# First product of an attention + feed-forward kernel: direct sums before, Strassen's 7 block products from the third chunk on

## The chip, the cores and the metric

One NeuronCore of a Trainium2 chip. The metric is the device time of one execution in microseconds (us). Before the change it was 1001.22 us (median of 3 runs, 1000.88 to 1002.4).

## What is computed

`q`, `k`, `v` are (8 batches, 8 heads, 576 tokens, 64). Each head has two attentions, and their outputs are added: one over tokens pooled by 4 (144 of them), repeated 4 times, and one in a band of 7 neighbours. The sum is laid out as `x` with 4608 rows (tokens) of 512, and then goes through a feed-forward layer without biases:

```python
h = x @ w_in                      # (4608, 512) @ (512, 2048): the first product
g = np.where(h >= 1, h, np.where(h <= -1, 0.0, (h + 1) ** 2 / 4))
return (g @ w_out).astype(np.float32)   # (4608, 2048) @ (2048, 512): the second product
```

All is in fp32. Each factor of the two large products is split into a high part in the fp32r format and the remainder ("low part", fp32r as well), and a product is the sum of three matmuls: high by high, low by high, high by low.

## The kernel before, in words

**Units of work.** The 2048 columns of `h` are cut into 16 slices `f` of 128. The tokens are cut into chunks `c`: 512, 256, and ten of 384. For each (chunk, slice) there is one step of the first product, `mm1` (L648): 12 matmuls 128x128 by 128 x chunk (4 blocks of the 512 input columns, 3 matmuls each, L663) into one PSUM bank. Then comes the activation with the split of its result (L675 to L696): Relu and Square on ScalarE, max/min on VectorE (L688), high part on ScalarE (L690), low part on VectorE (L695; on GpSimd in the first chunk, L692). Then `mm2` (L699) adds the slice's part of the second product into the chunk's output banks: for each 128 tokens 3 matmuls 128 x 512 (L714). After the last slice ScalarE copies the output to SBUF (L719) and SP's queue stores it (L720).

**Attention.** 32 units, one for each batch and pair of heads ("attention pair", L293): some 50 small matmuls in six steps (L369, L393, L493, L511, L534, L552) with VectorE, ScalarE and GpSimd work in between (GpSimd: L426, L479, L480). From the third batch on a pair uses the PSUM banks 0 to 2 (`shares`, L347). The last steps add the two attentions in PSUM (L577) and write the high and the low part of `x` (L592 on ScalarE, L597 on VectorE) into two rings of 1152 tokens, `xh` and `xl`.

**Weights.** `w_in` and `w_out` come from HBM as 64-bit words of doubles' bits, 512 KB for each slice and matrix (L619), and are converted on ScalarE and VectorE during the first chunk (L623 to L640). All 32 converted tiles then stay in SBUF.

**Order.** Nothing is ordered by hand: a planner (`Plan`, L81) has a cost, a due time (`key`) and the buffers of each operation, plays them through and writes out one fixed order for each engine; on the chip each engine, and SP's queue of transfers, goes through its own list in that order. `mm1` runs some 11 us ahead of `mm2` (`lead`). Attention of the first batch stands ahead of all, that of the second beside the first chunk, later ones beside the chunk ahead of the one that needs them.

## Time and profile before

| | |
|---|---|
| Median of the runs | 1001.22 us |
| The profiled execution's own time | 999.11 us |
| Its span, first to last instruction | 997.3 us |
| TensorE clock granted, mean over the span | 0.991 |
| PE / VectorE / ScalarE / GpSimd busy | 97% / 51% / 49% / 12% of the span |
| Moved by DMA | 66.23 MB |

The profile is one execution. PE is TensorE's matmuls, PEld its weight loads (they overlap matmuls), DVE VectorE, ACT ScalarE, POOL GpSimd, SP the queue that issues the transfers. Matmuls are pipelined: a row's duration is longer than the distance to the next row, and the price of a matmul is the distance from start to start. L with a number is a line of the kernel. A row of a timeline has start, duration, engine, line, operation, out<-in, shape, and how many were merged; a row of a window has its length and then each engine's busy time and count, the granted clock, the DMA engines' busy share and GB/s; a row of the groups has total, mean in ns, idle time before and what ended it.

### The profile page before, as it was taken

Reading aid. Unit: us, or ns where it says so; the run is one execution under the profiler, and the core shown is the slowest. Engines: PE = TensorE matmul, PEld = TensorE weight load, DVE = VectorE, ACT = ScalarE, POOL = GpSimd, SP = SyncE. Lnnn points to the kernel's source line nnn. Section 1 sums busy time; section 2 is a strip of 40 time slices with the busy share of each in tenths; the row PEclk is TensorE's granted clock in tenths of the full one; section 3 lists DMA queues with packets and bytes.
Section 4 is the critical chain, followed back from the end, with each engine's and each line's share of the span. In section 5 each row is a group of like instructions: output and inputs, shape, how many; then the busy total and the mean of one; then the engine's idle time right before and its main releaser. Section 6 shows DMA issues by size and latency. Waiting matters only on the chain.

```text
span 997.3 us, 18271 instructions
## 1 busy us (share of the span) xinstructions
PE 965.8 (97%) x7620; PEld 831.5 (83%) x7620; DVE 505.0 (51%) x908; ACT 485.3 (49%) x1063; POOL 123.5 (12%) x120
## 2 busy tenths in 40 slices
PE   7799999999999999999999999999999999999998
PEld 5577778888888888998887888998888888899997
...
DMA packets 26531, 66.23 MB, mean 66 GB/s; under 512 B 3152, under 2 KB 3152, under 8 KB 26448
## 3 DMA queue, kind: packets, MB, share of 16 engines
...
q14 instruction: 23, 0.19, 0.1%
...
## 4 chain that ended last, share of the span: by engine, by line
PE 84%; DVE 8%; ACT 3%; DMA 2%; issue 1%; SPq 0%; ACTq 0%; DVEq 0%
PE ps L714 38%; PE ps L663 37%; PE ps L369 2%; PE ps L511 2%; PE ps L493 2%; PE ps L534 2%; PE ps L552 1%; ACT sp L450 1%; PE ps L393 1%; DMA raw_i<-w_in 1%; DVE m L630 1%; DVE ps L460 1%; DMA vp<-vp 1%; DVE m L628 1%; DVE xl L597 1%
## 5 line engine op out<-in xcount | busy, mean ns | idle before, releaser
L663 PE MATMUL ps<-xh,w_i 128*128 128x384 f32 (+2 forms) x1536 | 396.3, 340 | 7.0 <-DVE gl L695 4.8
L714 PE MATMUL ps<-w_o,gh 128*128 128x512 f32 x1152 | 369.5, 402 | 0.5 <-DVE w_o L639 0.5
L663 PEld LDWEIGHTS ps<-xh,w_i 128*128 128x128 f32 x1536 | 275.2, 188 | 31.7 <-DVE gl L695 10.4
L663 PE MATMUL ps<-xl,w_i 128*128 128x384 f32 (+2 forms) x768 | 258.8, 337 | 0.0
L714 PEld LDWEIGHTS ps<-w_o,gh 128*128 128x128 f32 x1152 | 207.3, 188 | 43.0 <-issue 9.5
L714 PE MATMUL ps<-w_o,gl 128*128 128x512 f32 x576 | 227.4, 395 | 0.0
L688 DVE SCALAR_TENSOR_TENSOR ps<-ps,u 128x384 f32<-128x384 f32 (+1 forms) x176 | 96.5, 548 | 257.9 <-ACT u L680 257.9
L675 ACT ACTIVATE u<-ps 128x384 f32<-128x384 f32 (+2 forms) x192 | 94.4, 492 | 255.3 <-PE ps L663 255.3
L695 DVE TENSOR_TENSOR gl<-ps,gh 128x384 fp32r<-128x384 f32 (+1 forms) x176 | 95.9, 545 | 107.6 <-PE ps L714 64.3
L663 PEld LDWEIGHTS ps<-xl,w_i 128*128 128x128 f32 x768 | 144.6, 188 | 2.9
L690 ACT CAST gh<-ps 128x384 fp32r<-128x384 f32 (+1 forms) x176 | 83.1, 472 | 109.0 <-DVE ps L688 106.6
L714 PEld LDWEIGHTS ps<-w_o,gl 128*128 128x128 f32 x576 | 108.2, 188 | 25.2
L680 ACT ACTIVATE u<-u 128x384 f32<-128x384 f32 (+2 forms) x192 | 100.8, 525 | 6.0
L426 POOL TENSOR_TENSOR sl<-sl,mxl 128x640 f32<-128x640 f32 x24 | 30.3, 1261 | 468.5 <-DVE mxl L424 468.5
L479 POOL TENSOR_TENSOR vh<-vp 72x512 f32<-72x512 f32 x32 | 41.4, 1295 | 133.0 <-ACT u L675 57.9
L450 ACT ACTIVATE sp<-ps,mxp 128x144 f32<-128x144 f32 x96 | 36.4, 380 | 28.2 <-DVE ps L460 14.1
L421 DVE TENSOR_TENSOR sl<-ps,band_sb 128x640 f32<-128x640 f32 x24 | 19.8, 825 | 55.4 <-PE ps L393 49.5
L428 ACT ACTIVATE sl<-sl 128x640 f32<-128x640 f32 x32 | 23.6, 737 | 37.0 <-POOL sl L426 28.4
L460 DVE TENSOR_REDUCE ps<-sl 128x10 f32<-128x640 f32 x32 | 26.4, 826 | 16.1 <-ACT sp L450 13.8
L511 PE MATMUL ps<-ident,sp 128*72 128x128 f32 x192 | 27.4, 281 | 5.8 <-ACT al L499 5.1
L692 POOL TENSOR_TENSOR gl<-u,gh 128x512 fp32r<-128x512 f32 x16 | 22.6, 1411 | 78.8 <-ACT gh L690 61.1
L592 ACT CAST xh<-ps 128x576 fp32r<-128x576 f32 x32 | 20.4, 639 | 22.2 <-DVE ps L577 22.1
...
## 6 DMA issues: line engine op xcount, KB each, us to landing
...
```

Of the source, the lines that this page charges most:

```text
L426: o_s = op("POOL", 1.3, lambda: nc.gpsimd.tensor_tensor(slf(), slf(), ml_n(), op=ALU.subtract), [o_m], [slb, mlb], kk[2], name=name + "sub ...
L450: nc.scalar.activation(spb.tile[:, i], sp_view()[:, i] if i < 2 else sp_other(), AF.Exp, bias=mxb.tile[:, i : i + 1], scale=scale, accum_o ...
L460: o_su = op("DVE", 0.825, lambda: nc.vector.tensor_reduce(sums()[:, 0:NB], slf(), axis=AX.X, op=ALU.add), [o_e, o_sp], [slb, spp], kk[4], ...
L479: nc.gpsimd.tensor_tensor(vhb.tile, vpb.tile[:, :, 0:2, :], vpb.tile[:, :, 2:4, :], op=ALU.add)
L511: nc.tensor.transpose(tp_v[:, kb, i, :], spb.tile[:, i, kb * KB : (kb + 1) * KB], ident if i < 2 else swapped,)
L663: nc.tensor.matmul(h, wi[:, wt, cc * P : (cc + 1) * P], xt[:, cc, ts], start=(i == 0), stop=(i == 3 * NCC - 1))
L675: o2 = op("ACT", 0.49 + e, lambda: nc.scalar.activation(u(), h(), AF.Relu, bias=0.5, scale=0.5), [o1], [hb, ub], key, name=f"relu {c},{f}" ...
L680: nc.scalar.activation(u(), u(), AF.Square)
L688: o4 = op("DVE", 0.556 + e * 1.2, lambda: nc.vector.scalar_tensor_tensor(g(), h(), 1.0, u(), op0=ALU.max, op1=ALU.min), [o3], [hb, ub], ke ...
L690: o5 = op("ACT", 0.50 + e, lambda: nc.scalar.copy(ghb.tile[:, :n], g()), [o4], [held, ghb], key, name=f"gh {c},{f}")
L695: o6 = op("DVE", 0.556 + e * 1.2, lambda: nc.vector.tensor_tensor(glb.tile[:, :n], g(), ghb.tile[:, :n], op=ALU.subtract), [o5], [held, gh ...
L714: nc.tensor.matmul(o, g.tile[:, ts], wb.tile[:, wt, :], start=f == 0 and i == 0, stop=f == NFC - 1 and i == 2)
```

## The change

The chunks become nine of 512 tokens. The first two still use the direct product. From the third on two slices `f1`, `f2` = 2j, 2j+1 are taken together, and the 256x512 by 512x512 product is made of 2x2 blocks with Strassen's scheme in Winograd's form: A11, A12, A21, A22 are the blocks of the two slices' weights (slice, half of the 512 input columns), B11 to B22 those of `x` (half of the columns, half of the tokens). With S1 = A21+A22, S2 = S1-A11, S3 = A11-A21, S4 = A12-S2 and T1 = B12-B11, T2 = B22-T1, T3 = B22-B12, T4 = B21-T2 there are seven products (A11 B11, A12 B21, S2 T2, S3 T3, S1 T1, A22 T4, S4 B22) in place of eight. Each is 6 matmuls of 128x128 by 128x256 (L883).

- **Products** (`winograd`): they go by turns into two PSUM banks G and H, of which half is used. Two add on top of what stands there (S2 T2 and S1 T1 on A11 B11), S4 B22 as well. Between them ScalarE copies a bank to SBUF three times (L889), and VectorE adds a bank to such a copy three times (L892). The two banks change roles from one j to the next; the next j's first product waits for both.
- **Activation** (`hidden`): on four quarters of 256 tokens by 128 columns for each j instead of on whole chunks. Three quarters have their source in SBUF (`tt`), one in PSUM. The second product keeps its shape: 8 x 3 matmuls 128x512 for each j (L833).
- **Sums of x** (`sums_of_x`): attention writes `x` as fp32 into a ring `xr` of 1024 tokens (L591); for each chunk VectorE makes the four T (L688), ScalarE the high and VectorE the low parts of seven operands (L705, L706). L592 and L597 of before are gone. The first two chunks get plain high and low parts (`parts`).
- **Sums of weights** (`sums_of_weights`, `stored`): once for each j, beside the second chunk, VectorE makes S1 to S4 (L731), with high and low parts (L753); they and A11, A12, A22 are stored to HBM: A1 512 KB, A22 256 KB, S12 512 KB, S34 512 KB. Each chunk from the third on loads them again (L861), into 8 places of SBUF where w_in of the slices 0 to 7 had been; the operands of x take 12 places, 8 of them of w_in's slices 8 to 15.
- **Banks**: outputs have the banks 4 to 7, G and H the banks 2 and 3, attention the banks 0 and 1 (`shares` is off).
- The planner's due times and costs are set anew (`K`), and it now can give one operation several buffers of a pool.

The core of the diff (the lines of the changed kernel in the text above are those of its own numbering):

```diff
-RING = 2 * S
-
-CHUNKS = [(0, 512), (512, 256)] + [(t, 384) for t in range(768, NT, 384)]
-NCH = len(CHUNKS)
+TOK = 512
+NCH = NT // TOK
+DIRECT = 2
+RING = 2 * TOK
+HALF = TOK // 2
...
-    xh = cpool.tile([P, NCC, RING], F32R, name="xh")
-    xl = cpool.tile([P, NCC, RING], F32R, name="xl")
+    xr = cpool.tile([P, NCC, RING], F32, name="xr")
+    tt = cpool.tile([P, NT1, HALF], F32, name="tt")
+    gt = cpool.tile([P, NG1, 2 * HALF], F32R, name="gt")
     ps = ppool.tile([P, 8, 512], F32, name="ps")
+    dpool = ctx.enter_context(tc.tile_pool(name="dram", bufs=1, space=bass.MemoryType.DRAM))
...
-        shares = b > 1
+        shares = False
...
+                nc.vector.tensor_tensor(
+                    xr[:, p, r : r + m].rearrange("p (s f) -> p s f", f=FACTOR),
+                    pl_s()[:, s0 : s0 + m].rearrange("p (s f) -> p s f", f=FACTOR),
+                    xdb.tile[:, s0 // FACTOR : (s0 + m) // FACTOR].unsqueeze(2).broadcast_to([P, m // FACTOR, FACTOR]),
+                    op=ALU.add,
...
+        war = [o for c in range(NCH) if TOK * c <= S * b + S - RING - 1 for o in x_read[c][p]] if b > 1 else []
+        o_x = op("DVE", 0.755, add, [o_xd] + war, [plp, xdb], kk[9], name=name + "x")
+        x_done[b, p] = o_x
...
+    def parts(c):
+        for kt in range(NCC):
+            pb = sbuf("x", [P, 2, TOK], F32R, "w", [32 + kt])
+            src = xr[:, kt, r0 : r0 + TOK]
+            o1 = op("ACT", 0.62, lambda pb=pb, src=src: nc.scalar.copy(pb.tile[:, 0], src), deps, [pb], key + 0.3 * kt, name=f"xh {c},{kt}")
+            o2 = op("DVE", 0.69, lambda pb=pb, src=src: nc.vector.tensor_tensor(pb.tile[:, 1], src, pb.tile[:, 0], op=ALU.subtract),
+                    [o1], [pb], key + 0.3 * kt, name=f"xl {c},{kt}", port=True)
...
+    def sums_of_x(c):
...
+        order = ["B11", "B21", "T2", "T3", "T1", "T4", "B22"]
+        buf = {x: sbuf(x, [P, 2, 2, HALF], F32R, "w", list(EVEN) + list(XP)) for x in order}
...
+        t1 = diff("T1", lambda: raw(0, 1), lambda: raw(0, 0), last + done[0], [tmp["T1"], buf["T1"]], key["T2"])
+        t2 = diff("T2", lambda: raw(1, 1), lambda: low("T1"), done[1] + [t1], [tmp["T1"], tmp["T2"], buf["T2"]], key["T2"])
+        t4 = diff("T4", lambda: raw(1, 0), lambda: low("T2"), done[1] + [t2], [tmp["T2"], tmp["T4"], buf["T4"]], key["T4"])
+        t3 = diff("T3", lambda: raw(1, 1), lambda: raw(0, 1), last + done[0] + done[1], [tmp["T3"], buf["T3"]], key["T3"])
...
+        for x in order:
+            o1 = op("ACT", 0.62, lambda pb=pb, src=src: nc.scalar.copy(pb.tile[:, 0], src()), deps, [pb] + ([tmp[x]] if x in tmp else []), key[x], name=f"{x}h {c}")
+            o2 = op("DVE", 0.69, lambda pb=pb, src=src: nc.vector.tensor_tensor(pb.tile[:, 1], src(), pb.tile[:, 0], op=ALU.subtract),
+                    [o1] + need.get(x, []), [pb] + ([tmp[x]] if x in tmp else []), key[x], name=f"{x}l {c}", port=True)
...
+    def sums_of_weights(j):
...
+        s1 = op("SP", 1.31, lambda: nc.sync.dma_start(mem["A1"], w1().bitcast(F32)), d1, [r1], dkey, name=f"sA1 {j}")
+        s2 = op("SP", 0.8, lambda: nc.sync.dma_start(mem["A22"], w2()[:, :, 256:512].bitcast(F32)), d2, [r2], dkey, name=f"sA22 {j}")
...
+        a2 = op("DVE", 0.69, two(lambda: ta.tile, f32(r2, 0), f32(r2, 1), add), d2, [r2, ta, tb, tc_], key, name=f"wa2 {j}", port=True)
+        a1 = op("DVE", 0.69, two(lambda: tb.tile, f32(r1, 0), f32(r1, 1), add), d1, [r1, ta, tb, tc_], key, name=f"wa1 {j}", port=True)
+        q1 = op("DVE", 0.42, two(of(tc_, 0), of(ta, 0), of(ta, 1), add), [a2], [ta, tc_], key, name=f"wS1 {j}", port=True)
+        q2 = op("DVE", 0.42, two(of(tc_, 1), of(tc_, 0), of(tb, 0), sub), [q1, a1], [tb, tc_], key, name=f"wS2 {j}", port=True)
+        q3 = op("DVE", 0.42, two(of(ta, 0), of(tb, 0), of(ta, 0), sub), [q1, a1], [ta, tb], key, name=f"wS3 {j}", port=True)
+        q4 = op("DVE", 0.42, two(of(ta, 1), of(tb, 1), of(tc_, 1), sub), [q2, q1], [ta, tb, tc_], key, name=f"wS4 {j}", port=True)
+        free = [s1, s2, a1, a2, m1_ops[DIRECT - 1, f1], m1_ops[DIRECT - 1, f2]]
...
+            o1 = op("ACT", 0.62, cast, deps + free, [r, t], key, name=f"{x}h {j}")
+            o2 = op("DVE", 0.69, lambda: nc.vector.tensor_tensor(r.st[:, 1], t.tile, r.st[:, 0], op=sub), [o1], [r, t], key, name=f"{x}l {j}", port=True)
+            return op("SP", 1.31, lambda: nc.sync.dma_start(mem[x], r.st.bitcast(F32)), [o1, o2], [r], key, name=f"s{x} {j}")
...
+        s3 = staged(r1, tc_, [q1, q2], "S12")
+        s4 = staged(r2, ta, [q3, q4], "S34")
+        stored[j] = {"A1": (s1, mem["A1"], 1.31), "A22": (s2, mem["A22"], 0.75), "S12": (s3, mem["S12"], 1.31), "S34": (s4, mem["S34"], 1.31)}
...
+    def hidden(c, name, src, srcbuf, deps, n, key, pool=False):
+        e = {512: 0.11, 256: -0.13}[n]
+        v = {512: 0.69, 256: 0.42}[n]
+        sb = n == 256 and srcbuf.pool == "t"
+        o2 = op("ACT", 0.49 + e, lambda: nc.scalar.activation(u(), src(), AF.Relu, bias=0.5, scale=0.5), deps, [srcbuf, ub], key, name=f"relu {name}",
...
+        o3 = op("ACT", 0.52 + e, square, [o2], [ub], key, name=f"sq {name}")
+        g, held = (u, ub) if pool else (src, srcbuf)
+        o4 = op("DVE", v, lambda: nc.vector.scalar_tensor_tensor(g(), src(), 1.0, u(), op0=ALU.max, op1=ALU.min),
+                [o3], [srcbuf, ub], key, name=f"stt {name}", port=sb)
+        o5 = op("ACT", 0.50 + e, lambda: nc.scalar.copy(gb.tile[:, 0], g()), [o4], [held, gb], key, name=f"gh {name}")
...
+            o6 = op("DVE", v, lambda: nc.vector.tensor_tensor(gb.tile[:, 1], g(), gb.tile[:, 0], op=ALU.subtract),
+                    [o5], [held, gb], key, name=f"gl {name}", port=sb)
+        return gb, [o5, o6]
...
+    def winograd(c, j):
...
+        for x, (st, mem, cost) in stored[j].items():
+            n = 256 if x == "A22" else 512
+            lb[x] = sbuf("l" + x, [P, 2, n], F32R, "w", range(0, 16, 2))
+            ld[x] = op("SP", cost, lambda x=x, mem=mem: nc.sync.dma_start(lb[x].tile.bitcast(F32), mem), [st], [lb[x]], pos[c, f1] - K["sl"], name=f"l{x} {c},{j}")
...
+        G, H_ = psum([(2 + (j + c * (NFC // 2)) % 2,)]), psum([(3 - (j + c * (NFC // 2)) % 2,)])
+        g, h = (lambda: G.tile[:, 0, 0:HALF]), (lambda: H_.tile[:, 0, 0:HALF])
...
+            def run():
+                n = 0
+                for k in range(2):
+                    for w, v in ((0, 0), (1, 0), (0, 1)):
+                        nc.tensor.matmul(dst(), l(w, k), yb.tile[:, v, k], start=first and n == 0, stop=n == 5, skip_group_check=True)
+                        n += 1
+
+            return op("PE", 6 * 0.118, run, [ld[lname]] + yd + deps, [B_, lb[lname], yb] + list(extra), kk[i], name=f"M{x}{y} {c},{j}")
...
+        def copy(b, src, B_, o, i, name):
+            return op("ACT", 0.365, lambda: nc.scalar.copy(b.tile, src()), [o], [b, B_], kk[i], name=f"{name} {c},{j}")
+
+        def plus(b, src, B_, deps, i, name):
+            return op("DVE", 0.425, lambda: nc.vector.tensor_tensor(b.tile, src(), b.tile, op=ALU.add), deps, [b, B_], kk[i], name=f"{name} {c},{j}")
+
+        m1 = product(0, "A11", "B11", G, g, True, [], [H_])
+        c1 = copy(t1, g, G, m1, 0, "M1s")
+        m2 = product(1, "A12", "B21", H_, h, True, [m1])
+        p11 = plus(t1, h, H_, [m2, c1], 1, "C11")
+        m6 = product(2, "S2", "T2", G, g, False, [c1, m2])
+        c2 = copy(t2, g, G, m6, 2, "U2s")
+        m7 = product(3, "S3", "T3", H_, h, True, [p11, m6])
+        c7 = copy(t7, h, H_, m7, 3, "M7s")
+        m5 = product(4, "S1", "T1", G, g, False, [c2, m7])
+        p22 = plus(t7, g, G, [m5, c7], 4, "C22")
+        m4 = product(5, "A22", "T4", H_, h, False, [c7, m5])
+        p21 = plus(t2, h, H_, [m4, c2], 5, "C21")
+        m3 = product(6, "S4", "B22", G, g, False, [p22, m4])
+        quarters = [
+            (f1, 0, "11", (lambda: t1.tile), t1, [p11], 1),
+            (f2, HALF, "22", (lambda: t7.tile), t7, [p22], 4),
+            (f2, 0, "21", (lambda: t2.tile), t2, [p21], 5),
+            (f1, HALF, "12", g, G, [m3], 6),
+        ]
+        for f, tok, nm, src, held, deps, i in quarters:
+            gb, gdeps = hidden(c, f"{c},{j},{nm}", src, held, deps, HALF, kk[i])
+            second(c, f, gb, gdeps, tok, HALF, pos[c, f1] + K["nq"] * i, f"{c},{j},{nm}")
...
+        if c < DIRECT:
+            parts(c)
+            for f in range(NFC):
+                mm1(c, f)
+                mm2(c, f, 0, TOK)
+        else:
+            sums_of_x(c)
+            for j in range(NFC // 2):
+                if c == DIRECT:
+                    sums_of_weights(j)
+                winograd(c, j)
```

More of the change, by code (lines that the diff above doesn't have):

```diff
@@ L59 @@
 WARM = 10
-NW = 16
+NT1 = 10
+NG1 = 6
 class Buf:
@@ L134, in run, with pick @@
                 make_ready(o)
-        def pick(b):
+        def pick(b, taken):
             best = None
             for units in b.places:
-                if any((b.pool, u) in busy for u in units):
+                if any((b.pool, u) in busy or (b.pool, u) in taken for u in units):
                     continue
@@ L599, in attention @@
-        if not extra:
-            before.update(tl=o_tl, tp=o_tp, al=o_al, x=o_x)
-        x_done.setdefault(b, []).extend([o_xh, o_xl])
+            s0 = 0
+            while s0 < S:
+                r = (b * S + s0) % RING
+                m = min(S - s0, RING - r)
+                nc.vector.tensor_tensor(
[3 more added lines that the diff above has]
+                    op=ALU.add,
+                )
+                s0 += m
@@ L646, in attention_then_ffn @@
+    m1_ops = {}
     ob = {}
[L648 removed]
+    sums_done = {}
+    def hidden(c, name, src, srcbuf, deps, n, key, pool=False):
         op = plan.op
[L650 to L676 removed]
@@ L682, in square @@
                 nc.scalar.activation(u(), u(), AF.Square, bias=0.5, scale=0.5)
-        o3 = op("ACT", 0.52 + e, square, [o2], [ub], key, name=f"sq {c},{f}")
-        on_pool = c == 0 and f in GL_POOL(K)
-        g = u if on_pool else h
-        held = ub if on_pool else hb
-        o4 = op("DVE", 0.556 + e * 1.2, lambda: nc.vector.scalar_tensor_tensor(g(), h(), 1.0, u(), op0=ALU.max, op1=ALU.min),
-                [o3], [hb, ub], key, name=f"stt {c},{f}")
-        o5 = op("ACT", 0.50 + e, lambda: nc.scalar.copy(ghb.tile[:, :n], g()), [o4], [held, ghb], key, name=f"gh {c},{f}")
@@ new lines, in hidden, with mm1 @@
+        return gb, [o5, o6]
+    gd = {}
+    def mm1(c, f):
+        op = plan.op
+        wb, wd = weights["i", f]
+        key = pos[c, f] - K["lead"]
+        hb = psum([(2,), (3,)])
+        def run():
+            i = 0
+            for cc in range(NCC):
+                xt = part[c, cc][0].tile
+                for w, x in ((0, 0), (1, 0), (0, 1)):
+                    nc.tensor.matmul(hb.tile[:, 0, :], wb.tile[:, w, cc * P : (cc + 1) * P], xt[:, x], start=(i == 0), stop=(i == 3 * NCC - 1))
+                    i += 1
+        xd = [o for cc in range(NCC) for o in part[c, cc][1]]
+        o1 = op("PE", 12 * 0.228, run, xd + wd, [hb, wb] + [part[c, cc][0] for cc in range(NCC)], key, name=f"m1 {c},{f}")
+        m1_ops[c, f] = o1
+        gd[c, f] = hidden(c, f"{c},{f}", lambda: hb.tile[:, 0, :], hb, [o1], TOK, key, c == 0 and f in GL_POOL(K))
@@ L710, in run, with second @@
+    def second(c, f, gb, deps, t0, n, key, name):
+        op = plan.op
+        wb, wd = weights["o", f]
+        for t in range(t0 // P, (t0 + n) // P):
+            if (c, t) not in ob:
+                ob[c, t] = psum([(4 + t,)])
+                sums_done[c, t] = []
+            users = sums_done[c, t]
             def run(t=t):
+                i0 = done.setdefault((c, t), 0)
                 o = ob[c, t].tile[:, 0, :]
-                ts = slice(t * P, (t + 1) * P)
-                for i, (g, wt) in enumerate(((ghb, 0), (ghb, 1), (glb, 0))):
-                    nc.tensor.matmul(o, g.tile[:, ts], wb.tile[:, wt, :], start=f == 0 and i == 0, stop=f == NFC - 1 and i == 2)
@@ L722, in attention_then_ffn @@
-    for nxt in range(4):
-        attention(nxt)
+                ts = slice(t * P - t0, (t + 1) * P - t0)
+                for i, (g, w) in enumerate(((0, 0), (0, 1), (1, 0))):
+                    nc.tensor.matmul(o, gb.tile[:, g, ts], wb.tile[:, w, :], start=i0 + i == 0, stop=i0 + i == 3 * NFC - 1)
+                done[c, t] += 3
+            o1 = op("PE", 0.695, run, deps + wd, [gb, wb, ob[c, t]], key, name=f"m2 {name},{t}")
+            users.append(o1)
+            if len(users) == NFC:
+                osb = temp(2)
+                o2 = op("ACT", 0.58, lambda t=t, osb=osb: nc.scalar.copy(osb.tile, ob[c, t].tile[:, 0, :]), users, [osb, ob[c, t]], key, name=f"out {c},{t}")
+                a = c * TOK + t * P
+                op("SP", 0.7, lambda a=a, osb=osb: nc.sync.dma_start(out[a : a + P, :], osb.tile), [o2], [osb], key, name=f"st {c},{t}")
@@ L724, in attention_then_ffn @@
+    for n in range(NPAIR):
+        attention(n)
     for f in range(NFC):
@@ L726, in attention_then_ffn @@
         convert("o", f)
-    nxt = 4
     for c in range(NCH):
-        while nxt < len(pairs) and pairs[nxt][0] <= max(chunk_batches(c)):
-            attention(nxt)
-            nxt += 1
-        for f in range(NFC):
-            mm1(c, f)
-            mm2(c, f)
+        if c:
+            for n in range(c * NPAIR, min(c + 1, B) * NPAIR):
+                attention(n)
+        if c < DIRECT:
[3 more added lines that the diff above has]
+                mm2(c, f, 0, TOK)
+        else:
+            sums_of_x(c)
[3 more added lines that the diff above has]
+                winograd(c, j)
     total = plan.run()
```

213 lines of the change are left out of this document (119 added, 94 removed).

## Prediction

> **What bounds it now.** I read the page's parts 1 and 4, then windows by stage, then PE's timeline.
>
> ```profile
> span 997.3 us, 18271 instructions
> PE 965.8 (97%) x7620; PEld 831.5 (83%) x7620; DVE 505.0 (51%) x908; ACT 485.3 (49%) x1063; POOL 123.5 (12%) x120
> PE 84%; DVE 8%; ACT 3%; DMA 2%; issue 1%; SPq 0%; ACTq 0%; DVEq 0%
> ```
> ```profile
> 25.00:50.00 25.00, 18.07 (x241) 14.11 (x242) 22.05 (x40) 22.32 (x50) 3.15 (x3) 0.80 1.02 396
> 44.50:155.60 111.10, 104.26 (x771) 81.27 (x770) 100.42 (x158) 88.58 (x173) 30.00 (x23) 0.99 0.37 123
> 203.10:981.70 778.60, 772.72 (x5962) 676.67 (x5961) 353.96 (x652) 345.59 (x770) 76.71 (x70) 1.00 0.15 46
> ```
>
> 84% of the last chain is PE. In the 778.6 us of the 384-token chunks PE idles 5.9 us, 0.25 for each of the 24 attention pairs there, at full clock; DVE and ACT are under half busy. Only the first chunk (111.1 us) has DVE at 90%. So most of the time goes as PE's work does, whose prices are start-to-start distances:
>
> ```profile
> 153.09 0.63 PE L663 MATMUL ps<-xh,w_i 128*128 128x512 f32 x2
> ...
> 155.83 0.64 PE L714 MATMUL ps<-w_o,gh 128*128 128x512 f32 x2
> ...
> 158.60 0.40 PE L663 MATMUL ps<-xh,w_i 128*128 128x256 f32 x2
> ...
> 161.44 0.62 PE L714 MATMUL ps<-w_o,gh 128*128 128x512 f32 x2
> ...
> 207.12 0.62 PE L663 MATMUL ps<-xh,w_i 128*128 128x384 f32 x2
> ...
> 403.07 0.51 PE L663 MATMUL ps<-xh,w_i 128*128 128x384 f32 x2
> ...
> 405.19 0.62 PE L714 MATMUL ps<-w_o,gh 128*128 128x512 f32 x2
> ...
> 407.25 0.51 PE L663 MATMUL ps<-xh,w_i 128*128 128x384 f32 x2
> ...
> 984.53 0.51 PE L663 MATMUL ps<-xh,w_i 128*128 128x384 f32 x2
> ...
> 992.62 0.40 PE L714 MATMUL ps<-w_o,gl 128*128 128x512 f32 x1
> ```
>
> A step without attention takes 407.25-403.07 = 4.18 us (384 tokens, one slice). At 512 tokens it is 2.74 + 2.77 = 5.51. The 24 matmuls of 256 columns take 2.84: **0.118 us each**, one of 512 in the second product 2.77/12 = 0.231.
>
> **The change, part by part.**
>
> *PE's work.* In a stretch without attention its list, with the last slice pairs of the last chunk, was one step
>
> ```order
> L663 MATMUL ps<-xh,w_i_1527 128x384 x2
> L663 MATMUL ps<-xl,w_i_1527 128x384
> L663 MATMUL ps<-xh,w_i_1527 128x384 x2
> L663 MATMUL ps<-xl,w_i_1527 128x384
> L714 MATMUL ps<-w_o_1469,gh_9287 128x512 x2
> L714 MATMUL ps<-w_o_1469,gl_9301 128x512
> ```
>
> (part of a step), and is now one j (lA_51, lS_51 its weights, B_7 and T_7 the operands of x):
>
> ```order
> L883 MATMUL ps<-B_7_8342,lA_51_9841 128x256 x6
> L883 MATMUL ps<-B_7_8976,lA_51_9841 128x256 x6
> L883 MATMUL ps<-T_7_8999,lS_51_9905 128x256 x6
> L883 MATMUL ps<-T_7_9720,lS_51_9915 128x256 x6
> L833 MATMUL ps<-w_o_828,gt 128x512 x3
> L883 MATMUL ps<-T_7_8994,lS_51_9905 128x256 x6
> L883 MATMUL ps<-T_7_9733,lA_51_9881 128x256 x6
> L883 MATMUL ps<-B_7_8983,lS_51_9915 128x256 x6
> L833 MATMUL ps<-w_o_828,gt 128x512 x3
> L833 MATMUL ps<-w_o_782,gt 128x512 x6
> L833 MATMUL ps<-w_o_917,gt 128x512 x6
> ```
>
> One activation stood behind a whole step; now seven products share two banks, with 3 to 24 matmuls of the second product between them. One j: 42 x 0.118 + 24 x 0.231 = 4.96 + 5.54 = **10.50 us** for 512 tokens and two slices, 5.25 a slice, where 384-token steps took 4.18 x 512/384 = 5.57. There are 7 chunks x 8 = 56 of them: 588.0.
>
> [...]
>
> *Attention on PE.* From the first step of the third chunk (207.12) to the last (984.53) are 159 steps: 777.4 - 159 x 4.18 = 112.8, by 24 pairs 4.70 each, idle time included. Its matmuls stay; I keep 4.70.
>
> *Ends.* Chunk 1 starts at 158.60 and I keep that: attention loses L597 on 8 pairs and gains 4 x 0.67 of DVE work in `parts`, 3 us less on an engine 90% busy, against 6 MB of stores in SP's queue ahead of late raw weights. Bounds -3 and +4, taken 0. After the last product 18 matmuls of the second remain in PE's list (4.2), then 997.3 - 992.62 = 4.7 as now: 8.9.
>
> *Sum without new waits:* 158.6 + 16 x 5.51 (88.2) + 4 x 4.70 (18.8) + 588.0 + 20 x 4.70 (94.0) + 8.9 = **956.5**, against a span of 997.3.
>
> *DVE and ACT.* Prices of the pieces:
>
> ```profile
> L688 DVE SCALAR_TENSOR_TENSOR ps<-ps,u 128x384 f32<-128x384 f32 x160 | 89.7, 561 | 252.5 <-ACT u L680 252.5
> L695 DVE TENSOR_TENSOR gl<-ps,gh 128x384 fp32r<-128x384 f32 x160 | 89.1, 557 | 79.6 <-ACT gh L690 42.8 <-PE ps L714 36.4
> L597 DVE TENSOR_TENSOR xl<-ps,xh 128x576 fp32r<-128x576 f32 x32 | 24.1, 754 | 9.6 <-ACT xh L592 9.4
> L688 DVE SCALAR_TENSOR_TENSOR ps<-ps,u 128x256 f32<-128x256 f32 x16 | 6.8, 425 | 5.3 <-ACT u L680 5.3
> L680 ACT ACTIVATE u<-u 128x256 f32<-128x256 f32 x16 | 6.7, 419 | 0.5
> L675 ACT ACTIVATE u<-ps 128x256 f32<-128x256 f32 x16 | 6.1, 384 | 14.8 <-PE ps L663 14.8
> L690 ACT CAST gh<-ps 128x256 fp32r<-128x256 f32 x16 | 6.0, 372 | 11.1 <-DVE ps L688 10.5 <-PE ps L714 0.6
> L426 POOL TENSOR_TENSOR sl<-sl,mxl 128x640 f32<-128x640 f32 x24 | 30.3, 1261 | 468.5 <-DVE mxl L424 468.5
> L479 POOL TENSOR_TENSOR vh<-vp 72x512 f32<-72x512 f32 x32 | 41.4, 1295 | 133.0 <-ACT u L675 57.9 <-PE ps L534 57.2 <-issue 8.5
> L480 POOL TENSOR_TENSOR vd<-vh 72x256 f32<-72x256 f32 x32 | 24.2, 757 | 27.3 <-PE ps L552 25.2
> ```
>
> DVE now spends 354.0 - 160 x 1.118 = 175 us on 24 attention pairs, 7.3 each, 6.5 without L597. A chunk with attention will need 8 x 11 x 0.425 = 37.4, 4 x 6.5 = 26.2 and 11 x 0.67 = 7.4 for the sums of x: 71 us in the 8 x 10.50 + 18.8 = 102.8 of PE. ACT: a j has 3 x 0.372 + 4 x (0.384 + 0.419 + 0.372) = 5.8, 46.5 a chunk, and the rest adds about 20. Neither is the bound by sum. In the second chunk the sums of weights add 8 x (4 x 0.67 + 4 x 0.425) = 35 us to DVE; with 32 x 0.68 for the activations and the attention it stands near 91 of 107.
>
> *New waits.* Latencies, from a calm step:
>
> ```profile
> 405.01 0.34 PE L663 MATMUL ps<-xl,w_i 128*128 128x384 f32 x1
> ...
> 405.39 0.49 ACT L675 ACTIVATE u<-ps 128x384 f32<-128x384 f32 x1 [2.06 <-PE ps L663]
> ...
> 406.47 0.57 DVE L688 SCALAR_TENSOR_TENSOR ps<-ps,u 128x384 f32<-128x384 f32 x1 [2.55 <-ACT u L680]
> ...
> 407.07 0.48 ACT L690 CAST gh<-ps 128x384 fp32r<-128x384 f32 x1 [0.63 <-DVE ps L688]
> ```
>
> ACT starts 0.38 after the last matmul's start, 0.2 after its turn is over; DVE to ACT costs 0.03 (406.47+0.57 to 407.07). So G is free some 0.2 + 0.37 + 0.1 = 0.67 us after a product, and the product on H between takes 0.71: covered, by a hair. S4 B22 waits for an addition (0.2 + 0.43 + 0.1 = 0.73) behind one product of 0.71: 0.02 lost. The next j needs the bank of S4 B22, whose activation takes 0.2 + 0.38 + 0.42 + 0.43 + 0.37 + 0.43 = 2.2, against 18 matmuls (4.2 us): covered. In calm stretches a j thus loses almost nothing (I take 0.05). Beside attention one long instruction ahead in ACT's or DVE's list ends that cover. DVE's list there (some steps of the middle of the run, attention's L336, L464 to L468 among the activation's L688 and L695) was
>
> ```order
> L336 TENSOR_REDUCE qd_76<-q_5390 128x144
> L695 TENSOR_TENSOR gl_5440<-ps,gh_5436 128x384
> L464 TENSOR_SCALAR ps<-ps 128x13
> L465 RECIPROCAL ps<-ps 128x13
> L688 SCALAR_TENSOR_TENSOR ps<-ps,u_5438 128x384
> L468 TENSOR_TENSOR sl_5392<-sl_5392,ps 128x640
> L695 TENSOR_TENSOR gl_5464<-ps,gh_5462 128x384
> ```
>
> and in the fourth chunk is now (L892 adds G or H to a copy, L786 and L793 are the activation)
>
> ```order
> L892 TENSOR_TENSOR tt<-ps,tt 128x256
> L440 TENSOR_REDUCE mxl_4238<-sl_4200 128x10
> L352 TENSOR_REDUCE qd_76<-q_4198 128x144
> L786 SCALAR_TENSOR_TENSOR ps<-ps,tt 128x256
> L591 TENSOR_TENSOR xr<-ps,xd_4256 128x576
> L793 TENSOR_TENSOR gt<-ps,gt 128x256
> ```
>
> The long ones stand behind an addition that PE waits for (L892), not ahead of it, but each delay moves the rest. No row shows this kind of hand-over; lower bound 0, upper bound one long instruction (L597's 0.75) for each j beside attention. I take the 0.25 idle that an attention pair costs now, for each of the 40 j's beside attention: 10 us; 16 x 0.05 = 1; 2 for the second chunk's DVE (bounds 0 and 8). Sum: 956.5 + 13 = **969.5 span**.
>
> GpSimd can lengthen the new DVE work in SBUF:
>
> ```profile
> 82.11 0.67 DVE L639 TENSOR_TENSOR w_o<-m,w_o 128x512 fp32r<-128x512 f32 x1
> ...
> 84.47 0.82 DVE L418 TENSOR_TENSOR sl<-ps,mxl 128x640 f32<-128x640 f32 x1
> 85.22 1.28 DVE L639 TENSOR_TENSOR w_i<-m,w_i 128x512 fp32r<-128x512 f32 x1
> ```
> ```profile
> 84.64 1.31 POOL L692 TENSOR_TENSOR gl<-u,gh 128x512 fp32r<-128x512 f32 x1 [3.33 <-ACT w_i L635]
> ```
>
> The same L639 takes 0.67 alone and 1.28 while POOL works (until 85.95); L418, reading PSUM, keeps its 0.82. Six of a j's 11 DVE pieces now have both inputs in SBUF, where before none of a step's two had.
>
> *Streams.* 1.79 MB a j, at the 396 GB/s of the first row of windows 4.6 us in every 10.50; attention's 1.2 MB a pair adds 3. Loads have two sets of places, so a whole j of lead. They wait in SP's queue for their places, and attention's loads and the output's stores behind them wait too, but those are asked for well ahead: cost 0, until the rate falls below some 150 GB/s.
>
> The execution's own time was 999.11, 1.8 above its span; the runs' median 1001.22, 2.1 above that. 969.5 + 3.9 = **973**.
>
> **Rivals.**
>
> - *Delays by GpSimd.* It works 3.3 us per attention pair (1.26 + 1.30 + 0.76), 66 us beside the 40 j's. If each of these loses one more 0.6 us on PE's path: +24, 997. For: both inputs in SBUF. Against: only some pieces are waited for.
> - *The two banks bind: slower.* The gain is used up when each of the 40 j's loses 40.8/40 = 1.0 us. Place: G and H handed over behind the exponentials on ACT or sums on DVE. If two hand-overs of each j lose a long instruction, 40 x 1.5 = 60: 956.5 + 60 + 3 + 3.9 = 1023. Against it: PE's list has second-product work between. [...]
> - *Weight loads bind.* A product matmul then goes at the pace of its weight load, which lasts
>
> ```profile
> 158.72 0.19 PEld L663 LDWEIGHTS ps<-xl,w_i 128*128 128x128 f32 x1
> ```
>
>   0.19: 56 x 42 x (0.19 - 0.118) = +169, 1142: slower. [...] This row stands amid the matmuls that came every 0.118, so loads overlap.
> - *Loads late.* At 150 GB/s a j takes 12.2: +95, 1068. The rate was 396.
>
> **Chances.** Forecast 0.76; GpSimd 0.12; banks 0.10; the last two 0.01 each. Lower end: no new waits and 3 us off the first chunk, 956.5 - 3 + 3.9 = 957. Upper end: 0.75 on each of the 40 j's and 4 on the first chunk, 956.5 + 30 + 3 + 4 + 3.9 = 997, rounded up to 998; it takes in GpSimd's case. About 0.2% (2 us) can be told from no change. Faster by over 0.2% (under 999.2): the forecast, and 0.10 of GpSimd's case: 0.86; within it 0.02; slower 0.12.
>
> **What would show it.** Right: L883 rows 0.118 apart; a j without attention 10.5 to 10.7; PE idle under 0.5 per j beside attention; chunk 2 starting near 266. Wrong: idle time of PE ahead of L883 released by L889, L892 or L706; L786 or L793 above 0.5 us mean; idle PE released by lA or lS transfers; DVE over 95% in the second chunk with PE waiting.

## The result, and the profile after

The changed kernel takes **967.64 us** (median of 4 runs, 966.57 to 969.08) against 1001.24 (1000.88 to 1002.4) for the kernel before, run beside it: a ratio of 0.9663, with a 95% interval of 0.9646 to 0.9681. The profiled execution took 966.57, its span is 964.6.

The page's head and its chain of work that ended last:

```profile
span 964.6 us, 20765 instructions
...
PE 941.1 (98%) x8052; PEld 800.1 (83%) x8052; DVE 649.7 (67%) x1337; ACT 580.1 (60%) x1464; POOL 123.6 (13%) x120
...
PE 87%; DVE 6%; DMA 4%; ACT 2%; issue 0%; SPq 0%; ACTq 0%; DVEq 0%
```

PE is still what the time goes by, with 24.7 us less work (965.8 to 941.1), although it has 432 matmuls more. VectorE went from 51% to 67%. The same by stages: the first chunk, the second, the third, the next four, and the eighth. Columns: length, then busy time and count of PE, PEld, DVE, ACT, POOL, granted clock, DMA share, GB/s.

```profile
44.50:158.90 114.40, 110.16 (x867) 86.70 (x866) 106.17 (x171) 91.24 (x178) 31.22 (x24) 0.97 0.50 178
158.90:268.90 110.00, 108.48 (x841) 85.17 (x840) 90.63 (x162) 58.51 (x121) 14.42 (x13) 1.00 0.45 155
268.90:371.65 102.75, 102.68 (x967) 88.91 (x966) 71.25 (x162) 62.28 (x171) 13.25 (x12) 1.00 0.64 212
371.65:785.60 413.95, 413.37 (x3838) 358.25 (x3837) 274.60 (x607) 250.41 (x683) 49.54 (x45) 1.00 0.60 195
785.60:871.15 85.55, 85.55 (x529) 76.66 (x528) 39.76 (x95) 46.16 (x127) 0.00 (x0) 1.00 0.57 185
```

PE idles 0.07 us in the third chunk, 0.58 in the next four, nothing in the eighth. But busy time does not show what a j still loses: from 883.79 to 893.86 us PE is busy for all 10.07 us, while the prices of the matmuls in it add up to 9.81. That is seen in the distances from start to start. PE's timeline of this j, one without attention in the last chunk:

```profile
883.79 1.58 PE L883 MATMUL ps<-B,lA 128*128 128x256 f32 x12
885.21 1.74 PE L883 MATMUL ps<-T,lS 128*128 128x256 f32 x12
886.78 0.87 PE L833 MATMUL ps<-w_o,gt 128*128 128x512 f32 x3
887.49 0.88 PE L883 MATMUL ps<-T,lS 128*128 128x256 f32 x6
888.20 0.86 PE L883 MATMUL ps<-T,lA 128*128 128x256 f32 x6
888.89 0.94 PE L883 MATMUL ps<-B,lS 128*128 128x256 f32 x6
889.67 4.35 PE L833 MATMUL ps<-w_o,gt 128*128 128x512 f32 x18
893.86 0.52 PE L883 MATMUL ps<-B,lA 128*128 128x256 f32 x3
```

The first 12 product matmuls take 1.42 (0.118 each). The next 12, S2 T2 and S3 T3, take 1.57 to the next row: 0.15 too long. S4 B22 takes 0.78 in place of 0.71. VectorE's timeline says why:

```profile
885.48 0.42 DVE L892 TENSOR_TENSOR tt<-ps,tt 128x256 f32<-128x256 f32 x1 [2.20 <-PE ps L883]
```

S3 T3 goes into bank H, and could start at 885.21 + 0.71 = 885.92, but the addition that reads H (C11) ends at 885.90, and its handing over comes on top: by the row at 886.78, less the 0.71 of six matmuls, S3 T3 started at an estimated 886.07, 0.17 after the addition. So a j of 42 products and 21 second-product matmuls (the three that are missing here come at the chunk's end) takes 10.07 where 42 x 0.118 + 21 x 0.231 is 9.81.

### The profile page after: what moved, and what is told of

Same layout as the page of the kernel before. It is cut to its first block, busy times and chain, and to the rows that moved or that the text cites. A ratio compares the mean times of both kernels' runs of the same rounds, so it can differ in the third digit from the quotient of the medians.

```text
span 964.6 us, 20765 instructions
## 1 busy us (share of the span) xinstructions
PE 941.1 (98%) x8052; PEld 800.1 (83%) x8052; DVE 649.7 (67%) x1337; ACT 580.1 (60%) x1464; POOL 123.6 (13%) x120
## 4 chain that ended last, share of the span: by engine, by line
PE 87%; DVE 6%; DMA 4%; ACT 2%; issue 0%; SPq 0%; ACTq 0%; DVEq 0%
PE ps L833 39%; PE ps L883 29%; PE ps L810 8%; PE ps L385 2%; PE ps L527 2%; PE ps L409 2%; PE ps L550 2%; PE ps L509 2%; PE ps L568 2%; DMA q<-qT 1%; ACT sp L466 1%; DMA raw_i<-w_in 1%; DMA vp<-vp 1%; DVE ps L476 1%; DVE tt L630 1%; DVE tt L632 1%
## 5 line engine op out<-in xcount | busy, mean ns | idle before, releaser
L833 PE MATMUL ps<-w_o,gt 128*128 128x512 f32 x1728 | 441.3, 398 | 0.0
L833 PEld LDWEIGHTS ps<-w_o,gt 128*128 128x128 f32 x1728 | 310.2, 188 | 63.7 <-issue 5.0
L883 PE MATMUL ps<-T,lS 128*128 128x256 f32 x1008 | 144.8, 285 | 0.3
L883 PEld LDWEIGHTS ps<-T,lS 128*128 128x128 f32 x1008 | 131.9, 188 | 9.3 <-ACT tt L889 2.1
L892 DVE TENSOR_TENSOR tt<-ps,tt 128x256 f32<-128x256 f32 x168 | 70.0, 421 | 101.7 <-PE ps L883 96.0
L889 ACT COPY tt<-ps 128x256 f32<-128x256 f32 x168 | 59.0, 369 | 106.8 <-PE ps L883 105.8
L780 ACT ACTIVATE tt<-tt 128x256 f32<-128x256 f32 (+1 forms) x256 | 113.0, 444 | 6.8
L786 DVE SCALAR_TENSOR_TENSOR tt<-tt 128x256 f32<-128x256 f32 x168 | 77.9, 465 | 46.2 <-ACT tt L780 45.1
L810 PE MATMUL ps<-x,w_i 128*128 128x512 f32 x384 | 95.9, 400 | 0.0
L883 PEld LDWEIGHTS ps<-B,lA 128*128 128x128 f32 x672 | 87.9, 188 | 7.9 <-issue 2.8
L883 PE MATMUL ps<-B,lA 128*128 128x256 f32 x672 | 94.4, 284 | 0.0
L788 ACT CAST gt<-tt 128x256 fp32r<-128x256 f32 (+1 forms) x184 | 76.8, 421 | 26.4 <-DVE tt L786 24.8
L793 DVE TENSOR_TENSOR gt<-tt,gt 128x256 fp32r<-128x256 f32 x168 | 71.6, 431 | 18.7 <-ACT gt L788 15.8
L883 PE MATMUL ps<-T,lA 128*128 128x256 f32 x336 | 50.1, 284 | 0.0
L883 PE MATMUL ps<-B,lS 128*128 128x256 f32 x336 | 49.9, 284 | 0.0
L883 PEld LDWEIGHTS ps<-T,lA 128*128 128x128 f32 x336 | 44.0, 188 | 2.9 <-ACT sl L444 0.8
```

What stands on the lines that cost most here:

```text
L780: nc.scalar.activation(u(), u(), AF.Square)
L786: o4 = op("DVE", v, lambda: nc.vector.scalar_tensor_tensor(g(), src(), 1.0, u(), op0=ALU.max, op1=ALU.min), [o3], [srcbuf, ub], key, name= ...
L788: o5 = op("ACT", 0.50 + e, lambda: nc.scalar.copy(gb.tile[:, 0], g()), [o4], [held, gb], key, name=f"gh {name}")
L793: o6 = op("DVE", v, lambda: nc.vector.tensor_tensor(gb.tile[:, 1], g(), gb.tile[:, 0], op=ALU.subtract), [o5], [held, gb], key, name=f"gl ...
L810: nc.tensor.matmul(hb.tile[:, 0, :], wb.tile[:, w, cc * P : (cc + 1) * P], xt[:, x], start=(i == 0), stop=(i == 3 * NCC - 1))
L833: nc.tensor.matmul(o, gb.tile[:, g, ts], wb.tile[:, w, :], start=i0 + i == 0, stop=i0 + i == 3 * NFC - 1)
```

## The experiments

The time before is that of the runs made beside the kernels (medians 1000.3 to 1000.8). "From the third chunk on" is from its first product's start to the end of the span: 268.9 to 964.6 in the changed kernel, 695.7 us.

**All chunks by the direct product** (the chunk size and the ring stay).

```diff
-DIRECT = 2
+DIRECT = 9
```

> All nine chunks of 512 tokens by the direct product; no block products, no sums of weights, the ring of x as it is. Theory (the block products pay by their smaller count of matmuls, the larger chunk only a little): 158.9 to chunk 1, then 8 chunks of 16 x 5.51 = 705.6, 24 attention pairs of 4.70 = 112.8, end 8.9: span 986, time about 990, so 22 us above the changed kernel and 11 below the kernel before. Rival (the chunk of 512 tokens and the ring of x bring the gain): 965 to 972, as the changed kernel.

Measured: 1000.64, ratio 0.9995 to 1.0022 against the kernel before: no gain at all. Its third chunk, the eighth and the ninth by windows (same columns):

```profile
281.70:389.70 108.00, 107.63 (x830) 84.68 (x829) 52.68 (x93) 46.79 (x97) 13.12 (x12) 1.00 0.17 55
...
819.40:909.00 89.60, 88.87 (x385) 72.06 (x385) 24.54 (x36) 33.38 (x57) 0.00 (x0) 1.00 0.03 12
909.00:1002.80 93.80, 89.06 (x385) 71.87 (x384) 22.24 (x32) 32.13 (x54) 0.00 (x0) 0.99 0.06 21
```

A chunk with attention takes 108.0 against 102.75 and 103.5 (413.95/4) of the changed kernel, one without 89.6 against 85.55; from the third chunk on 721.1 against 695.7, 25.4 more. The rival falls: the block products bring the gain. The theory's total of 990 was missed all the same: the planner lists this kernel's first chunk in another order, and that chunk ends 12.6 us later (171.5 against 158.9). After the first chunk this kernel is 7.4 faster than the kernel before (1002.8 - 171.5 against 997.3 - 158.6), which is put down here to 512 tokens in place of 384 and the ring; the two were not tried apart. So 997.3 to 964.6 divides into 25.4 for the block products and 7.4 for chunk and ring, with next to nothing over. One caution: the profiled run, 1004.65, was 4 above this kernel's median; if those 4 us lay behind the third chunk's start, the block products' part is 21.

**One chunk more by the direct product**, with the sums of weights moved along.

```diff
-DIRECT = 2
+DIRECT = 3
...
-        key = pos[1, f2] + K["sw"]
-        dkey = pos[1, f2] + K["sd"]
+        key = pos[DIRECT - 1, f2] + K["sw"]
+        dkey = pos[DIRECT - 1, f2] + K["sd"]
```

> One chunk more by the direct product (block products from the fourth chunk on; the sums of weights move one chunk on with them). Theory (a chunk by block products gains what its count of matmuls says, 88.2 against 84.0, less some waits; all-direct chunks cost 25.4 us more over seven): 3 to 5 us above the changed kernel from the third chunk's start to the end, 970 to 973 in all if the first two chunks stay as they are. Rival (the gain is in the second chunk or in the chunk of 512 tokens): no more than 967.6.

Measured: 981.53, 14 us above. Its second and third chunk by windows, PE's longest wait there, and VectorE's timeline up to its end:

```profile
160.00:270.00 110.00, 109.58 (x850) 86.36 (x849) 61.04 (x109) 49.53 (x105) 13.42 (x13) 1.00 0.19 57
270.00:382.60 112.60, 106.66 (x810) 83.49 (x809) 80.06 (x145) 52.83 (x110) 14.62 (x12) 0.97 0.43 149
```
```profile
PE ps L810 <- DVE gt L793: 5.0, 2, 4.4
```
```profile
276.87 0.82 DVE L437 TENSOR_TENSOR sl<-ps,band_sb 128x640 f32<-128x640 f32 x1 [6.19 <-ACT S34s L750]
...
278.53 0.68 DVE L753 TENSOR_TENSOR S12s<-tt,S12s 128x512 fp32r<-128x512 f32 x1
279.13 1.75 DVE L753 TENSOR_TENSOR S34s<-tt,S34s 128x512 fp32r<-128x512 f32 x1
...
282.81 0.68 DVE L793 TENSOR_TENSOR gt<-ps,gt 128x512 fp32r<-128x512 f32 x1
```

The rival falls, but the theory's size was wrong too: from the third chunk on 707.2, 11.5 more and not 3 to 5. The third chunk now is a direct one that also carries the sums of weights: 113.2 from start to start where a direct one without them takes 108.0 (direct9) and one of block products 102.7. So of the 11.5 some 5.3 are the direct product itself and 5.2 the sums beside it. PE waits there 4.4 us in one piece for an activation (L793), which stands in VectorE's list behind two sums of weights (L753) and what follows them. VectorE was not short of time: it had stood idle for 6.2 us just before, at attention's L437, with the sums and the activation behind it in its list. So the 5 us are read as the order of the lists here, and no run tried another order; in the changed kernel the second chunk, which carries them, is no longer (110.0) than direct9's second without (110.2).

**The hand-over copies doubled**: all three of a j, the first alone, the other two alone.

```diff
-            return op("ACT", 0.365, lambda: nc.scalar.copy(b.tile, src()), [o], ...
+            return op("ACT", 0.365, lambda: [nc.scalar.copy(b.tile, src()) for _ in range(2)], [o], ...
```

(the first alone: `range(2 - (i > 0))`, the others alone: `range(1 + (i > 0))`; the planner's cost, so the order of all lists, is unchanged)

> Each ScalarE copy that hands a bank over (L889) is issued twice; the lists are as they were, each hand-over 0.37 us later. Theory of the prediction (the copy of G is covered by a hair, 0.67 against the 0.71 of the product on H): S2 T2 starts 0.33 later in each of the 56 j's, less the 0.15 that S3 T3 then no longer waits: 10 to 18 us more, 978 to 986; the other two copies of a j have three second-product matmuls ahead of the product that needs them and stay hidden. Rival (the hand-over has slack): under 3 us more. Rival (hand-overs beside attention stand behind long instructions already): over 30 more.

> Only the first of a j's three copies (of G, between A11 B11 and S2 T2) is issued twice. Doubling all three cost 16 us. Theory (only this one binds, with 0.04 us to spare; the others have three matmuls of the second product ahead of the product that needs them): 14 to 17 us above the changed kernel, 981 to 985. Rival (each of the three costs about a third): about 973.

> The other two copies of a j (of G after S2 T2, of H after S3 T3) are issued twice, the first once. Theory: hidden, within 3 us of the changed kernel, 966 to 970. Rival (each copy costs about a third of the 16 us of all three): about 978.

Measured: 983.72 with all, **977.59** with the first, **977.53** with the others. The sum for all three had come out as the theory had it (16 us), but for a wrong reason: the first costs 10 and not 14 to 17, and the two that I called hidden cost 10 as well; together they cost less than both apart. By place: a j without attention goes from 10.03 to 10.32 with the first copy doubled, but the fifth chunk, with attention, only from 103.9 to 105.05, 0.15 a j. That chunk's j's are of two kinds. In three of them nothing but A12 B21 stands between A11 B11 and S2 T2, and each loses 0.4; in the other five some of attention's matmuls stand there as well, and they lose nothing. Waits of PE's weight loads for such a copy, in the changed kernel from 268.9 us on and with the first copy doubled (us in total, times, longest):

```profile
PEld ps L883 <- ACT tt L889: 2.2, 5, 0.5
```
```profile
PEld ps L883 <- ACT tt L889: 13.1, 35, 0.5
```

PE's and VectorE's timelines of a j without attention, the two later copies doubled:

```profile
893.53 1.71 PE L883 MATMUL ps<-T,lS 128*128 128x256 f32 x12
895.08 0.85 PE L833 MATMUL ps<-w_o,gt 128*128 128x512 f32 x3
895.84 0.98 PE L883 MATMUL ps<-T,lS 128*128 128x256 f32 x6
896.66 0.85 PE L883 MATMUL ps<-T,lA 128*128 128x256 f32 x6
897.62 0.98 PE L883 MATMUL ps<-B,lS 128*128 128x256 f32 x6
```
```profile
896.81 0.42 DVE L793 TENSOR_TENSOR gt<-tt,gt 128x256 fp32r<-128x256 f32 x1 [1.23 <-ACT gt L788]
897.15 0.82 DVE L892 TENSOR_TENSOR tt<-ps,tt 128x256 f32<-128x256 f32 x2
```

S1 T1 starts 2.31 after S2 T2, against 2.28 before, and S1 T1 to A22 T4 is 0.82 (0.71 before): so the doubled copies were almost hidden, but not quite, 0.14. The larger part is that A22 T4 to S4 B22 is 0.96 (0.69 before). S4 B22 waits for an addition that by an estimate is free to start at some 896.75 (S1 T1's start at 895.84, its 0.71, and the 0.20 that lie between A22 T4's start and that addition's in the changed kernel, 888.20 to 888.40) and stands in VectorE's list behind L793, which waits for L788, which in ScalarE's list stands behind the doubled copies. By this reading most of the delay went round by a piece of activation that has nothing to do with that product.

**The same doubling with the activation of C11 keyed one place later.**

```diff
-            (f1, 0, "11", (lambda: t1.tile), t1, [p11], 1),
+            (f1, 0, "11", (lambda: t1.tile), t1, [p11], 2),
```

> The two later copies of a j doubled, as in the run that cost 10 us, but the activation of C11 is keyed one place later in the planner: ScalarE's list then has the copy of G between that activation's two pieces, and VectorE's has the addition that S4 B22 waits for ahead of C11's last piece (L793), not behind it. Theory (the 10 us come from the place in the two lists: addition behind L793 behind L788 behind the copies): 967 to 972. Rival (the doubled copies themselves come too late for the products): 976 to 979.

Measured: 987.83, worse than either expected. The planner answered on PE's list too:

```profile
900.23 2.86 PE L883 MATMUL ps<-T,lS 128*128 128x256 f32 x18
903.08 0.96 PE L883 MATMUL ps<-T,lA 128*128 128x256 f32 x6
903.87 0.84 PE L883 MATMUL ps<-B,lS 128*128 128x256 f32 x6
```
```profile
903.17 0.42 DVE L892 TENSOR_TENSOR tt<-ps,tt 128x256 f32<-128x256 f32 x1 [0.36 <-PE ps L883]
903.52 0.42 DVE L793 TENSOR_TENSOR gt<-tt,gt 128x256 fp32r<-128x256 f32 x1
```

Two things changed at once. On VectorE the addition stands ahead of L793, as intended, and S4 B22 follows A22 T4 after 0.79 and not 0.96: so the place in the lists did make most of that wait. But S2 T2, S3 T3 and S1 T1 now stand side by side and take 2.85 in place of 18 x 0.118 = 2.12: without the three second-product matmuls between them S1 T1 meets the doubled copies with no cover but S3 T3. So the total, 10 us above the run with the same copies and the list before, does not separate what the run was meant to. How much of these 10 us is the lost cover stays open, since this order of the lists was not run with single copies.

**Less work for GpSimd.**

```diff
-            ... nc.gpsimd.tensor_tensor(slf(), slf(), ml_n(), op=ALU.subtract)
+            ... nc.gpsimd.tensor_tensor(slf()[:, 0:2], slf()[:, 0:2], ml_n()[:, 0:2], op=ALU.subtract)
...
-            nc.gpsimd.tensor_tensor(vhb.tile, vpb.tile[:, :, 0:2, :], vpb.tile[:, :, 2:4, :], op=ALU.add)
-            nc.gpsimd.tensor_tensor(vdb.tile, vhb.tile[:, :, 0, :], vhb.tile[:, :, 1, :], op=ALU.add)
+            nc.gpsimd.tensor_tensor(vdb.tile, vpb.tile[:, :, 0, :], vpb.tile[:, :, 1, :], op=ALU.add)
```

> GpSimd's work in attention is cut from 3.3 to about 1.0 us a pair: the maxima are subtracted from 128 of 640 columns only, and the pooled v is the sum of two of its four slices (that part of attention's result is left out). Theory (GpSimd lengthens VectorE's pieces, 465 against 428 ns, but PE waits for few of them): from the third chunk's start to the end 0 to 2 us less than the 695.7 of the changed kernel; up to 4 less before it, where VectorE is the bound. Rival (PE's waits beside attention are GpSimd's): 5 us less or more from the third chunk on.

Measured: 964.66, with GpSimd at 1.2 us a pair (0.40 + 0.78). The third chunk starts 2.3 earlier (266.6), and from there to the end it is 696.1 against 695.7: nothing. The activation's piece with both inputs in SBUF, of the changed kernel and of this one (here the line is 785):

```profile
L786 DVE SCALAR_TENSOR_TENSOR tt<-tt 128x256 f32<-128x256 f32 x168 | 77.9, 465 | 46.2 <-ACT tt L780 45.1
```
```profile
L785 DVE SCALAR_TENSOR_TENSOR tt<-tt 128x256 f32<-128x256 f32 x168 | 72.9, 436 | 46.0 <-ACT tt L779 45.2
```

So GpSimd's work does lengthen it, by 29 ns in the mean, and from the third chunk on it makes the kernel no slower.

**The streamed bytes doubled**, first into the same place, then by a copy from memory to memory that nothing waits for.

```diff
-            ld[x] = op("SP", cost, lambda ...: nc.sync.dma_start(lb[x].tile.bitcast(F32), mem), ...
+            ld[x] = op("SP", cost, lambda ...: [nc.sync.dma_start(lb[x].tile.bitcast(F32), mem) for _ in range(2)], ...
```
```diff
+            ld[x] = op("SP", cost, lambda ...: [nc.sync.dma_start(lb[x].tile.bitcast(F32), mem), nc.sync.dma_start(dpool.tile(...), mem)], ...
```

> Each load of a j's weights and sums of weights (lA, lS) is issued twice into the same place: 3.6 MB a j in place of 1.79. Theory (two sets of places give a whole j of lead, and at 396 GB/s 3.6 MB take 9.1 us of a j's 10.5 to 13): hidden in most j's, under 8 us more, 966 to 975. Rival (a load starts only when its place is free, late in the j before, and is waited for already when it takes twice as long): 30 us more or more, with PE's waits ahead of L883 released by lA or lS transfers.

> Each load of a j's weights (lA, lS) is followed by a copy of the same bytes from memory to another place in memory, which nothing waits for: the same 3.6 MB a j on the transfer engines, without a wait in SP's queue. Theory (the 434 us that doubling in place cost were SP's queue, in which each second load waited for the first to land; the transfers themselves have a j's lead): 967 to 975. Rival (the transfers' rate is what binds): 1010 or more, with PE's waits ahead of L883 released by lA or lS.

Measured: **1401.61** in place, **993.42** beside. SP's queue of the first:

```profile
SPq L861 <- DMA lA<-A: 467.5, 112, 6.9
SPq L861 <- DMA lS<-S: 411.3, 112, 5.1
```

and what PE waited for there:

```profile
PE ps L883 <- DMA lS<-S: 87.6, 32, 4.2
```

The second load into a place waits in the queue until the first has landed, 4 us each, 879 us in all or 15.7 for each j, more than the 10 that PE needs for one. So the sum is the queue's and not the bytes': DMA's share was only 59%. In the second run nothing waits for the copy. Its third chunk and its eighth, PE's longest wait in total, and VectorE's wait for attention's q from 273 to 815 us, here and in the changed kernel (us in total, times, longest):

```profile
273.40:382.00 108.60, 104.71 (x967) 89.98 (x966) 72.03 (x163) 62.12 (x171) 13.03 (x12) 0.98 0.92 336
...
815.30:901.80 86.50, 85.83 (x530) 76.56 (x529) 39.77 (x95) 46.11 (x127) 0.00 (x0) 1.00 0.95 353
```
```profile
PE ps L409 <- DVE xr L591: 12.2, 9, 2.5
```
```profile
DVE qd L352 <- DMA q<-qT: 42.9, 17, 4.5
```
```profile
DVE qd L352 <- DMA q<-qT: 15.3, 16, 1.7
```

In place the theory missed, and the rival's signs came: far over 30 us more, and PE waiting ahead of L883 for lS. Its reason was half right, since a place's load did take twice as long, but by waiting in the queue. Beside, both missed: 993 lies between them, and a wait of PE for lA or lS ahead of a product is no more than 0.2 us (of the 18.9 us that PE idled from 273.4 to 982 us, 18.7 are put down to others). Without attention a chunk takes 86.5 against 85.55 at a DMA share of 0.95: the products' own loads keep their lead even then. With attention it takes 108.4 in the mean of five against 103.3: attention's q, behind them in the queue and on the engines, comes late, VectorE waits for it, and PE waits for VectorE (12.2 us ahead of L409, in the changed kernel 2.2). Of the 30.7 us between the two spans 25.2 lie in these five chunks (273.4 to 815.3 us), 4.5 before them and 1.0 behind. So at the 185 to 212 GB/s of the changed kernel no product waits for its streams, and when bytes double it is attention's loads that come late first.

**Second-product matmuls between S2 T2 and S3 T3.** The planner is given a longer cost for an addition than it has on the chip (0.60, where L892 takes 0.42 us in the rows above); it then fills the gap.

```diff
-            return op("DVE", 0.425, lambda: nc.vector.tensor_tensor(b.tile, src(), b.tile, op=ALU.add), ...
+            return op("DVE", 0.60, lambda: nc.vector.tensor_tensor(b.tile, src(), b.tile, op=ALU.add), ...
```

> The planner takes 0.60 in place of 0.425 us for an addition (L892), so that PE's list has three second-product matmuls between S2 T2 and S3 T3 and between S1 T1 and A22 T4, where S2 T2 and S3 T3 stood side by side; the work is the same. Theory (what a j still loses, some 0.2 us in a calm one and 0.1 beside attention, is PE waiting for the addition ahead of S3 T3 and S4 B22): 16 x 0.2 + 40 x 0.1 = 7 us less, 958 to 963. Rival (the loss is in the matmuls' pace, or the waits come back at other hand-overs): within 2 us of 967.6.

> The same edit as before (0.60 in the planner for an addition), once more beside the changed kernel: 4 to 5 us below it (it gave 963.05). Rival (chance of one chip): within 2 us of it.

> The changed kernel as it is, beside the kernel before and the next three: 967.6.

Measured: 963.05, and once more, beside the changed kernel, 963.56 (ratio to before 0.9611 to 0.9641) against 967.33 (0.965 to 0.9687). The intervals are apart: this version beats both kernels, by 0.4% and 3.7%. PE's timeline of a j without attention:

```profile
881.61 1.57 PE L883 MATMUL ps<-B,lA 128*128 128x256 f32 x12
883.02 0.91 PE L883 MATMUL ps<-T,lS 128*128 128x256 f32 x6
883.76 0.85 PE L833 MATMUL ps<-w_o,gt 128*128 128x512 f32 x3
884.45 1.56 PE L883 MATMUL ps<-T,lS 128*128 128x256 f32 x12
885.86 0.84 PE L833 MATMUL ps<-w_o,gt 128*128 128x512 f32 x3
...
892.10 0.40 PE L883 MATMUL ps<-B,lA 128*128 128x256 f32 x2
```

Now the j takes 10.49 with 24 second-product matmuls, and 42 x 0.118 + 24 x 0.231 is 10.50: it loses nothing. From the third chunk on it takes 691.5, 4.2 less, of which 2.2 in the last two chunks and 2.0 in the five with attention. The rival falls. The size, 7 expected, was somewhat high, since a j beside attention gained 0.05 and not the 0.1 I had put there, and one without 0.14 and not 0.2.

## Why the prediction was right, point by point

- **PE's work as the bound, 0.118 and 0.231 a matmul**: right. A j without waits took 10.49 in the last experiment, the predicted 10.50. Twelve product matmuls in a row, with other weights each time, take 1.42, while one of their weight loads lasts 0.188 us (median of L883's): the loads overlap the matmuls, and the rival of the weight loads is dead.
- **Start of the second chunk**: 158.6 predicted, 158.89 measured, and in part by luck. The working put VectorE's work ahead of it at 3 us less; from 44.5 us to the second chunk's start VectorE was busy 102.2 us in the kernel before and 106.2 in the changed one, 4 more, which its idle time took up. **The second chunk**: 107 and 2 of waiting for VectorE, measured 110.0; VectorE's load there was predicted at 91 us and is 90.6, and in a later chunk 71 predicted, 71.25 measured.
- **No new waits without attention (0.05 a j)**: too low. From the eighth chunk's start (785.6) to the end are 179.0; 168 + 8.9 = 176.9 were predicted, so 2.1 over 16 j's, 0.13 each. From row to row it is 0.18, since the end hid 0.8: from the last matmul's start to the end of the span are 4.1 us, where the 8.9 held 4.7 and counted that matmul's 0.23 once more. The working had looked at G ("covered, by a hair") and at S4 B22; it had left out that S3 T3 waits for the addition on H in the same way, and there the cover (0.71) is shorter than the addition with its hand-overs (0.86 in the j shown, from 885.21 to the estimated 886.07). The last experiment took just that away: a j of its eighth and ninth chunk loses 0.02 in the mean.
- **New waits beside attention (0.25 a j, 10 us)**: this is the term that was mis-sized, and the only large miss. From 268.9 to 785.6 are 516.7 where 514 were predicted without waits: 2.7 in 40 j's, **0.07 each** (0.10 for equal work, since 954 second-product matmuls ran there and not the 960 of the sum). I had taken the idle time of an attention pair before for want of a row. What the runs showed in its place: beside attention the cover is longer, not shorter. A first copy later by 0.37 costs 0.29 a j without attention and 0.15 beside it, and there only those j's pay that have none of attention's matmuls between A11 B11 and S2 T2. That long instructions on ScalarE and VectorE stand ahead of a hand-over happens, but seldom. From 268.9 to the end PE's weight loads for products waited 2.2 us for a copy, in five places, and for an addition (us in total, times, longest):

```profile
PEld ps L883 <- DVE tt L892: 0.9, 5, 0.2
```

- **The end**: 8.9 predicted behind the last product with 18 matmuls of the second. There were 42 left, since most j's without attention do 21 and not 24 of them; the sum is untouched, because the j's before are shorter by as much.
- **What the miss adds up to**: 6.2 less than the 11 forecast for waits from the third chunk on (4.0 of it are waits, 1.4 the six matmuls fewer, 0.8 the end), 1.3 more in the first two chunks, and a median 1.1 above the profiled run and not 2.1: 973 against 967.6.
- **Rival GpSimd**: the lengthening is real (465 ns, 436 with less work on GpSimd) and worth nothing on PE's path from the third chunk on. **Rival of the two banks**: did not come true at 0.10 to 0.18 a j, but it was the right place to look: one copy 0.37 later costs 10 us, and with second-product matmuls as cover in two more places 4 us came back. With two banks the cover came short by 0.15 us at S3 T3, and three second-product matmuls put there made it up. **Rival of late loads**: nothing at the rate of this kernel; no wait of PE for lA or lS is in its trace. The bound of 150 GB/s was too low by the prediction's own figures (1.79 MB in 10.5 us are 170), but the measured 185 lies above both.
- **Where the gain comes from**: the 5.25 against 5.57 us a slice put 0.9 us a chunk on its size and 4.2 on the block products. Measured in direct9: 7.4 us over eight chunks, 4.05 in a chunk without attention and some 5 in one with it.
